# Swapping the operands of the query projection and building the identity first, in a decode attention kernel for one core

## The chip, the cores and the metric

The kernel runs on one core of a Trainium2 chip (trn2). The metric is the device time of one execution in microseconds (us), median over runs. A trace covers the "span" of the core, which is about 1.9 us shorter than the time. PE is the matmul engine, PEld its weight loads, DVE the vector engine, ACT the scalar engine, POOL GpSimd, SP the engine that issues the large loads. `SPq` lines are issues of DMA transfers. The traces also give the clock that PE was granted, as a share of full speed; here it lies between 0.50 ("the low clock" below) and 1.00. At the start of a trace it reads 1.00 although matmuls run slowly (last section); there "the low clock" means matmuls that run slowly, as where four K transposes take 1.09 us, against 0.64.

## The reference

Two independent attention decode steps (A over 8192 cached keys, B over the last 2048), one query token, batch 4, 32 query heads, 8 key/value heads of dimension 128, all bf16:

```python
q = (x @ wq).reshape(B, 1, 32, 128)           # x: [4, 1, 512], wq: [512, 4096]
scores = einsum(q, k) * 128 ** -0.5            # k, v repeated 4x over the heads
o = einsum(softmax(scores), v)
out = o.reshape(B, 1, 4096) @ wo               # wo: [4096, 512]
# the outputs of A and B are concatenated: [4, 1, 1024]
```

Every cached key and value, and every weight, is read from HBM once: 184.56 MB.

## The kernel before

The work is 20 "units" of 4 MB of K and 4 MB of V each: first four of B, then sixteen of A. K and V have two buffers each. For each unit PE transposes K (64 matmuls in 16 jobs), multiplies it with the query matrix RQ, and multiplies V with the exponentials. Ahead of this come the two query projections, problem 1 (B) first. Their weights lie in the V buffers until V is loaded. The parts that matter here:

```python
def pe_job_QP(P, i):                  # projection, a quarter of the heads
    def fn(pe):
        for hl in range(HQJ):         # 8 heads
            hq = i * HQJ + hl
            for c in range(DC):       # 4 chunks of 128
                pe.matmul(out=bk[:, hl * Bn:(hl + 1) * Bn], lhsT=wv[:, c, hq * DH:(hq + 1) * DH],
                          rhs=xT[:, P, c, :], start=(c == 0), stop=(c == DC - 1))
    # ... ACT copies bk to QT; pe_job_perm then reorders QT, and ACT writes RQ

# POOL, in this order: masks; memsets of ones, RQ, OT_sb, oacc, PT, Wo_sb; ident, identf; permE
def pool_setup1(pool):
    pool.affine_select(out=ident[:, :], in_=onesb[:, :], ...)     # waits for all the memsets

# SP: the loads of K and V
w = [("T", tjob_idx[(u - 2, 4 * q + 3)])] if u >= 2 else []       # K of unit u, piece q (B)
w = [("otr", u - 2)] if u >= 2 else [("T", tjob_idx[(1, 1)])] if u else [("T", qp_idx[(1, NQP - 1)])]   # V of unit u
# ... order on SP: WQ B, WQ A, K0, K1, V0, K2, V1, K3, V2, ...
```

SP issues loads in a fixed order (K0 is the K of unit 0, and so on). V0 waits for the end of problem 1's projection. K2 waits, in four pieces, for the transposes of unit 0. V1 waits for a transpose of unit 1. So a late PE makes SP issue late.

Of the kernel before, what the change touches and what calls it, by code (L numbers as in the profile page):

```python
# [9 lines left out]
ACTF = mybir.ActivationFunctionType  # L10
# [4 lines left out]
def bass_concat_heads__gqa_block_cached__sliding_block_cached__decode_kernel(  # L15
# [15 lines left out]
    Bn, _, D = A_x.shape  # L31
    _, HKV, SK, DH = A_k_cache.shape
    HQ = A_wq.shape[1] // DH
# [3 lines left out]
    DC = D // 128  # L37
# [6 lines left out]
    TC = NT // NC  # L44
    assert REP == 4 and Bn == 4 and HKV == 2 * NSEG and W == 64 * TS and NT == 128
    BIG = 1.0e30
    NQP = 4
    HQJ = HQ // NQP
    scale = float(DH) ** -0.5
    NKT = 4  # L50
    NW = 64
# [20 lines left out]
    with ExitStack() as es:  # L72
# [8 lines left out]
        def sm(name):  # L81
# [5 lines left out]
        Wo_sb = sb("Wo_sb", [128, C, D], BF16)  # L87
        Wl_sb = sb("Wl_sb", [128, C, D], BF16)
        ident = sb("ident", [128, 128], BF16)
        onesb = sb("onesb", [128, 128], BF16)  # L90
        identf = sb("identf", [128, 128], F32)
        onesf = sb("onesf", [128, 128], F32)
        RQ = [sb("RQ%d" % P, [128, Bn, NSEG, 2, 2 * C], BF16) for P in range(2)]
        RQc = sb("RQc", [128, 2, NSEG, 2, 2 * C], BF16)
        permE = sb("permE", [128, 2, 2, 64], BF16)
# [12 lines left out]
        xT = sb("xT", [128, 2, DC, Bn], BF16)  # L108
        QT = sb("QT", [128, 2, Bn, HQ], BF16)
        Dt = sb("Dt", [128, NT * C], F32)  # L110
        PT = sb("PT", [128, 2, NT * C + NW], BF16)
# [6 lines left out]
        oacc = sb("oacc", [Bn, D], F32)  # L118
# [6 lines left out]

        names = ["k0", "k1", "kh", "v0", "v1", "vl0", "vl1", "vl2", "vl3", "vl4", "wl0", "wl1", "wl2", "wl3", "wl4", "wl5", "wl6", "wl7", "x0", "x1", "w0", "w1", "wo",
                 "out0", "out1", "out2", "Tq", "Td", "Ta", "S", "PV", "Ed", "Ea", "Eq", "vs", "sub", "exp", "otr", "otp",
                 "ocp", "Ef", "fin0", "fin1", "ar1", "SM", "msk", "pset", "setup", "pm0", "pm1", "oc", "ocB", "mk0", "mk", "mka", "perm", "rq"]
        sems = {n: sm("s_" + n) for n in names}

        K_sbf = K_sb.bitcast(F32)
# [1 line left out]
        jobs = []  # L133
        bank_last = {}
        follow = {}
        tjob_idx, qp_idx, xt_idx, perm_idx, ot_idx, ol_idx, opj_idx = {}, {}, {}, {}, {}, {}, {}

        def sem_of(key):
            t = key[0]
# [26 lines left out]
        def op(eng, fn, waits=(), inc=None, bump=None):  # L166
            waits = list(waits)
            if not (eng == "pe" and turn[0] is not None):
                waits = [w for w in waits if w is not None]
            t = turn[0] if eng == "pe" or (eng in ("dve", "act") and turn[0] is not None and turn[0] >= T0P) else None  # L170
            plan[eng].append(dict(fn=fn, waits=waits, inc=inc, turn=t, bump=bump))

        def add(d):
            op(d["eng"], d["fn"], waits=d["waits"], inc=d["inc"])

        def new_job(kind, eng):
            idx = len(jobs)
            step = 2 if kind == "OT" else 1
            bank = (jobs[-1]["bank"] + step) % NBK if jobs else 0
            jobs.append(dict(kind=kind, idx=idx, bank=bank, prev=bank_last.get(bank), eng=eng, turn=turn[0]))  # L180
            bank_last[bank] = idx
            return idx

        def bankfree(idx):
            p = jobs[idx]["prev"]
            if p is None or (jobs[idx]["turn"] is not None and jobs[p]["turn"] is None):
                return None
            return ("F", p)

        def kbank(idx):  # L190
            return KTB[jobs[idx]["bank"]]
# [21 lines left out]
        def pe_job_QP(P, i):  # L213
            idx = qp_idx[(P, i)] = new_job("QP", "act")
            bk = kbank(idx)
            wv = wq_view(P)

            def fn(pe):
                ins = None
                for hl in range(HQJ):  # L220
                    hq = i * HQJ + hl
                    for c in range(DC):
                        ins = pe.matmul(out=bk[:, hl * Bn:(hl + 1) * Bn], lhsT=wv[:, c, hq * DH:(hq + 1) * DH],
                                        rhs=xT[:, P, c, :], start=(c == 0), stop=(c == DC - 1))
                return ins
            op("pe", fn, waits=[("WQ", P), ("E", xt_idx[P]), bankfree(idx)], inc=("T", idx))

            def efn(act):
                return act.activation(out=QT[:, P, :, i * HQJ:(i + 1) * HQJ],
                                      in_=bk[:, 0:HQJ * Bn].rearrange("p (h b) -> p b h", b=Bn), func=ACTF.Copy)  # L230
            add(dict(eng="act", fn=efn, waits=[("T", idx)], inc=("E", idx)))

        def pe_job_perm(P):
            idx = perm_idx[P] = new_job("perm", "act")
            bk = kbank(idx)

            def fn(pe):
                ins = None
                for e in range(2):
                    ins = pe.matmul(out=bk[:, e * Bn * HQ:(e + 1) * Bn * HQ],  # L240
                                    lhsT=permE[:, e, :, :].rearrange("p t i -> p (t i)"),
                                    rhs=QT[:, P, :, :].rearrange("p b h -> p (b h)"), start=True, stop=True)
                return ins
            op("pe", fn, waits=[("E", qp_idx[(P, NQP - 1)]), ("perm",), bankfree(idx)], inc=("T", idx))

            def efn(act):
                ins = None
                for tl in range(2):
                    ins = act.activation(
                        out=RQ[P][64 * tl:64 * tl + 64, :, :, :, C * tl:C * tl + C].rearrange("p b g e c -> p e (b g) c"),  # L250
                        in_=bk[64 * tl:64 * tl + 64, 0:2 * Bn * HQ].rearrange("p (e s c) -> p e s c", e=2, c=C), func=ACTF.Copy)
                return ins
            add(dict(eng="act", fn=efn, waits=[("T", idx)], inc=("E", idx)))

        def pe_filler(n):
            bank = (jobs[-1]["bank"] + 1) % NBK
# [34 lines left out]
        def pool_rq(u):  # L291
            un = units[u]
            w = [("E", perm_idx[un["P"]])]
            if un["P"] == 1:
                src = RQ[1][:, un["b"], :, :, :]
            else:
                src = RQ[0][:, un["b"], un["gp"]:un["gp"] + 1, :, :].broadcast_to([128, NSEG, 2, 2 * C])
            return dict(eng="pool", fn=lambda pool: pool.tensor_copy(out=RQc[:, u % 2, :, :, :], in_=src), waits=w, inc=("rq", u))
# [202 lines left out]
        def pool_otp(tn):  # L501
# [5 lines left out]
                w.append(("otr", 2 * tn - 2))  # L507
            return dict(eng="pool", fn=lambda pool: pool.tensor_copy(out=OTp[:, :, :], in_=OT_sb[:, P, q, :, :]), waits=w, inc=("otp", tn))

        def pool_mask0(pool):  # L510
            mkv = MK[:, :].rearrange("p (g s h) -> p g s h", g=NSEG, s=2)
            pool.memset(mkv[0:64, :, 0, :], 0.0)
            pool.memset(mkv[0:64, :, 1, :], -BIG)
            pool.memset(mkv[64:128, :, 0, :], -BIG)
            return pool.memset(mkv[64:128, :, 1, :], 0.0)
        op("pool", pool_mask0, inc=("mk0",))

        def pool_mask1(pool):
            pool.memset(MASK[0][0:64, 0:REP], 0.0)
# [2 lines left out]
            return pool.memset(MASK[0][64:128, REP:C], 0.0)  # L522
        op("pool", pool_mask1, inc=("mka",))

        def pool_setup0(pool):
            pool.memset(dummy[:, :], 0.0)
            pool.memset(onesf[:, :], 1.0)
            pool.memset(onesb[:, :], 1.0)
            pool.memset(RQ[0][:, :, :, :, :], 0.0)
            pool.memset(RQ[1][:, :, :, :, :], 0.0)  # L530
            pool.memset(OT_sb[:, :, :, :, :], 0.0)
            pool.memset(oacc[:, :], 0.0)
            pool.memset(PT[:, :, :], 0.0)
            return pool.memset(Wo_sb[:, :, :], 0.0)
        op("pool", pool_setup0, waits=[("mk0",), ("mka",)], inc=("pset",))

        def pool_setup1(pool):
            ins = pool.affine_select(out=ident[:, :], in_=onesb[:, :], pattern=[[1, 128]],
                                     compare_op=AluOpType.is_equal, fill=0.0, base=0, channel_multiplier=-1)
            ins = pool.affine_select(out=identf[:, :], in_=onesf[:, :], pattern=[[1, 128]],  # L540
                                     compare_op=AluOpType.is_equal, fill=0.0, base=0, channel_multiplier=-1)
            return ins
        op("pool", pool_setup1, waits=[("pset",)], inc=("setup",))

        def pool_perm(pool):
            ins = None
            for e in range(2):
                for tl in range(2):
                    ins = pool.tensor_copy(out=permE[:, e, tl, :], in_=ident[:, :].rearrange("p (i e) -> p e i", e=2)[:, e, :])
            return ins  # L550
        op("pool", pool_perm, waits=[("setup",)], inc=("perm",))
        def dve_msk(dve):
            idv = ident[0:NR, 0:NR].rearrange("p (h b) -> p h b", h=C)
            dve.tensor_reduce(out=MSK[:, :], in_=idv, axis=AX.X, op=AluOpType.max)
# [22 lines left out]
        for P in (1, 0):  # L577
            pe_job_xT(P)
            for i in range(NQP):
                pe_job_QP(P, i)  # L580
            pe_job_perm(P)
        op("pe", None, waits=[("E", perm_idx[0]), ("setup",), ("msk",)])
        op("dve", None, waits=[("msk",)])
        add(pool_rq(0))

        LA = 3
# [348 lines left out]
```

## Time and profile before

| | |
|---|---|
| time, median of 3 runs | 439.83 us (439.62 to 440.04) |
| span of the traced run | 437.9 us |
| bytes moved, mean rate | 184.75 MB, 422 GB/s |
| PE, DVE, ACT, POOL busy | 83%, 48%, 44%, 7% |

The page of the kernel before: engines, then 40 slices of 10.9 us each (a digit is the busy share in tenths), then what the DMA moved.

```profile
PE 363.9 (83%) x7174; PEld 336.5 (77%) x7184; DVE 209.5 (48%) x404; ACT 193.3 (44%) x217; POOL 29.1 (7%) x96
PE   0078898998998959896989598969878895989986
DMA  8999999999999999999999999999999999999996
GB/s 336 431 412 418 419 419 419 421 445 406 450 431 431 417 445 431 434 428 431 434 434 428 432 434 431 428 434 431 406 456 431 431 428 434 431 431 410 446 407 253
```

The DMA row is full between its first and last slice; no engine is. PE does nothing in the first two slices, and that is where the change works.

The timeline of the kernel before, first 38 us (start us, duration us, engine, line, operation, output and inputs, how many merged, and in brackets the idle time before and what ended it):

```profile
5.43 3.51 POOL L534 MEMSET Wo_sb<- 128x4096 bf16 x1
20.41 0.28 POOL L538 TENSOR_SCALAR_AFFINE_SELECT ident<-onesb 128x128 bf16<-128x128 bf16 x1 [11.47 <-issue]
21.10 0.26 PE L200 MATMUL KT<-ident,x_sb 4*128 4x4 bf16 x4 [21.10 <-POOL identf L540]
21.72 3.55 PE L223 MATMUL KT<-xT,V_sb 128*128 128x4 bf16 x128 [0.36 <-ACT xT L206]
27.12 3.66 PE L223 MATMUL KT<-xT,V_sb 128*128 128x4 bf16 x128 [0.94 <-ACT xT L206]
34.09 3.67 PE L279 MATMUL KT<-identf,K_sb 128*128 128x128 f32 x16 [2.62 <-DMA K_sb<-in_B_k_cache_dram]
37.82 1.09 PE L279 MATMUL KT<-identf,K_sb 128*128 128x128 f32 x4
```

POOL stands idle for 11.47 us before the identity. PE cannot start until that is there. Both projections are over by 31 us. Then PE waits for the first K, which lands at 34 us. So even here something slower than the projections ends the start-up: the loads.

The queue of SP in the same trace, from the first V load on:

```profile
25.31 3.80 SPq L568 DMA_DIRECT2D V_sb<-in_B_v_cache_dram  x4
37.79 10.35 SPq L568 DMA_DIRECT2D K_sb<-in_B_k_cache_dram  x4
55.68 2.48 SPq L568 DMA_DIRECT2D V_sb<-in_B_v_cache_dram  x4
58.27 6.93 SPq L568 DMA_DIRECT2D K_sb<-in_B_k_cache_dram  x4
```

The third of these lines is V1. When it is issued, 25.17 MB (WQ twice, K0, K1, V0, K2, at 4.19 MB each) have been issued and, summing the windows of 5 us, about 22.4 MB have moved. The remaining 2.7 MB last some 6.5 us at 420 GB/s. That is the stock that the DMA lives on while it waits for PE.

### The profile page before, as it was taken

To read this page: it belongs to the slowest core of one execution; us is meant where nothing else is said; L and a number is where in the kernel's file an instruction comes from. 1 tells how busy PE (TensorE), PEld (TensorE's weight loads), DVE (VectorE), ACT (ScalarE), POOL (GpSimd) and SP (SyncE) were. 2 spreads that over 40 slices of the span, in tenths; PEclk is the share of its full clock that TensorE was granted. 3 is DMA by queue.
4 is the path that set the end of the run, shared out by engine and by line. 5 is a ranking of instruction groups with operands and counts; after the bars stand their busy time and mean duration, and the time that the engine had idled before them with its cause. 6 is when DMAs were issued, how large, how long until landed. Compare 5 with 4: busy or idle time off the path is not lost.

```text
span 437.9 us, 15510 instructions
## 1 busy us (share of the span) xinstructions
PE 363.9 (83%) x7174; PEld 336.5 (77%) x7184; DVE 209.5 (48%) x404; ACT 193.3 (44%) x217; POOL 29.1 (7%) x96
## 2 busy tenths in 40 slices
PE   0078898998998959896989598969878895989986
PEld 0068897997997959795979588968868795979975
DVE  0004455664565634463456247625644563556641
ACT  1033473563653625372635264534534361635630
POOL 7110000000000000000000000000100000000000
PEclk9999999999999997999899699989998999999999
DMA  8999999999999999999999999999999999999996
GB/s 336 431 412 418 419 419 419 421 445 406 450 431 431 417 445 431 434 428 431 434 434 428 432 434 431 428 434 431 406 456 431 431 428 434 431 431 410 446 407 253
DMA packets 12500, 184.75 MB, mean 422 GB/s; under 512 B 1428, under 2 KB 2504, under 8 KB 2760
## 3 DMA queue, kind: packets, MB, share of 16 engines
q1 hardware_dynamic: 12400, 184.56, 99.2%
q8 instruction: 8, 0.13, 0.1%
q14 instruction: 4, 0.03, 0.0%
q0 software_dynamic: 64, 0.02, 0.0%
q10 hardware_dynamic: 24, 0.01, 0.0%
HBM read 184.56 MB, written 0.01 MB: 421 GB/s over the span
## 4 chain that ended last, share of the span: by engine, by line
PE 51%; DMA 43%; issue 2%; DVE 1%; SPq 1%; PEld 1%; PEldq 0%
DMA K_sb<-in_A_k_cache_dram 29%; PE KT L279 25%; PE OT L326 10%; DMA K_sb<-in_B_k_cache_dram 7%; DMA V_sb<-in_A_v_cache_dram 7%; PE SB L310 4%; PE SA L310 4%; PE KT L384 4%; SPq L568 1%; PE SA L338 1%; DVE oacc L392 1%; PE KT L326 1%; PEld OT L326 1%; PE KT L262 0%; DVE OS L489 0%
## 5 line engine op out<-in xcount | busy, mean ns | idle before, releaser
L279 PE MATMUL KT<-identf,K_sb 128*128 128x128 f32 x1280 | 206.2, 294 | 44.0 <-DMA K_sb<-in_A_k_cache_dram 33.0
L288 ACT ACTIVATE KT_sb<-KT 128x1024 bf16<-128x1024 bf16 x160 | 163.4, 1025 | 121.1 <-PE KT L279 121.1
L279 PEld LDWEIGHTS KT<-identf,K_sb 128*128 128x128 f32 x1280 | 146.2, 148 | 49.4 <-DMA K_sb<-in_A_k_cache_dram 34.2
L287 DVE COPY KT_sb<-KT 128x512 int32<-128x512 int32 x160 | 110.5, 690 | 131.2 <-PE KT L279 129.9
L326 PE MATMUL OT<-PT,V_sb 128*128 128x64 bf16 x2560 | 78.1, 193 | 2.5 <-issue 1.4
L326 PEld LDWEIGHTS OT<-PT,V_sb 128*128 128x128 bf16 x2560 | 75.9, 98 | 2.7 <-issue 1.5
L457 ACT ACTIVATE PT<-Dt 128x512 bf16<-128x512 f32 x40 | 24.6, 632 | 84.1 <-DVE Dt L446 84.1
L310 PEld LDWEIGHTS SA<-RQc,KT_sb 128*128 128x128 bf16 x1280 | 56.7, 98 | 2.3
L310 PEld LDWEIGHTS SB<-RQc,KT_sb 128*128 128x128 bf16 x1280 | 51.1, 97 | 7.9 <-issue 4.4
L310 PE MATMUL SA<-RQc,KT_sb 128*128 128x16 bf16 x1280 | 56.2, 170 | 0.0
L310 PE MATMUL SB<-RQc,KT_sb 128*128 128x16 bf16 x1280 | 52.8, 170 | 0.0
L408 DVE TENSOR_REDUCE M<-SB 128x8 f32<-128x512 f32 (+1 forms) x20 | 13.8, 692 | 49.9 <-PE SB L310 49.9
L429 POOL PARTITION_ALL_REDUCE MB<-M1m x20 | 7.7, 387 | 333.3 <-DVE M1m L422 333.3
L384 PE MATMUL KT<-Wo_sb,OL 128*4 128x512 bf16 x80 | 18.9, 379 | 0.0
L200 PE MATMUL KT<-ident,x_sb 4*128 4x4 bf16 x8 | 0.6, 170 | 21.1 <-POOL identf L540 21.1
L200 PEld LDWEIGHTS KT<-ident,x_sb 4*128 4x128 bf16 x8 | 0.4, 113 | 21.3 <-issue 21.3
L464 DVE TENSOR_REDUCE LB<-SA 128x8 f32<-128x512 f32 (+1 forms) x20 | 13.7, 684 | 2.8 <-PE SA L338 2.8
L446 DVE TENSOR_TENSOR Dt<-SA,MBm 128x512 f32<-128x512 f32 x20 | 13.8, 692 | 0.7
L355 DVE TENSOR_TENSOR ORx<-KT,MSK 32x1024 bf16<-32x1024 bf16 x10 | 12.1, 1211 | 3.7 <-PE KT L350 3.7
L408 DVE TENSOR_REDUCE M<-SA 128x8 f32<-128x512 f32 (+1 forms) x20 | 13.6, 681 | 0.0
L446 DVE TENSOR_TENSOR Dt<-SB,MBm 128x512 f32<-128x512 f32 x20 | 13.6, 681 | 0.0
L338 PE MATMUL SA<-PT,onesb 128*128 128x128 bf16 x168 | 12.7, 218 | 0.0
(74 smaller groups left out, 119.7 us busy)
## 6 DMA issues: line engine op xcount, KB each, us to landing
K_sb<-in_A_k_cache_dram SPq DMA_DIRECT2D x15, 4096.0 KB, 22.6
V_sb<-in_A_v_cache_dram SPq DMA_DIRECT2D x15, 4096.0 KB, 30.6
K_sb<-in_B_k_cache_dram SPq DMA_DIRECT2D x16, 1024.0 KB, 22.0
V_sb<-in_B_v_cache_dram SPq DMA_DIRECT2D x16, 1024.0 KB, 18.4
V_sb<-in_B_wq_dram SPq DMA_DIRECT2D x1, 4096.0 KB, 12.5
V_sb<-in_A_wq_dram SPq DMA_DIRECT2D x1, 4096.0 KB, 22.0
Wo_sb<-in_B_wo_dram SPq DMA_DIRECT2D x4, 1024.0 KB, 11.9
K_sb<-in_A_k_cache_dram SPq DMA_DIRECT2D x2, 2048.0 KB, 18.9
```

The lines of the kernel that those rows point to most:

```text
L279: ins = pe.transpose(out=bkf[:, pi * 128:(pi + 1) * 128], in_=K_sbf[:, slot, t0:t0 + 2, :].rearrange("p t d -> p (t d)"), identity=identf[ ...
L287: return e.tensor_copy(out=KT_sb.bitcast(I32)[:, tj % NKT, :], in_=bkf.bitcast(I32)[:, :])
L288: return e.activation(out=KT_sb[:, tj % NKT, :], in_=bk[:, :], func=ACTF.Copy)
L310: ins = pe.matmul(out=stb[:, t % NTH * C:(t % NTH + 2) * C], lhsT=ktv[:, pi, :, e], rhs=RQc[:, u % 2, t // TS, e, :], start=(e == 0), stop ...
L326: ins = pe.matmul(out=otb[:, s * NW:s * NW + w], lhsT=V_sb[:, slot, t, :], rhs=PT[:, slot, t * C:t * C + w], start=(j == 0), stop=(j == n ...
L338: ins = pe.matmul(out=SA[u % 2][:, s * NM:(s + 1) * NM], lhsT=onesb[:, :], rhs=PT[:, u % 2, c0:c0 + NM], start=(i == 0), stop=(i == n - 1))
L355: return dve.tensor_tensor(out=ORx[:, :, :, :], in0=bk[0:NR, 0:128].rearrange("p (i o r) -> p r o i", o=1, r=C).broadcast_to([NR, C, C, 12 ...
L384: ins = pe.matmul(out=bk[0:Bn, 0:D], lhsT=OL[:, i, :], rhs=Wo_sb[:, i, :], start=(i == 0), stop=(i == C - 1))
L408: return dve.tensor_reduce(out=M1[:, h * n:(h + 1) * n].rearrange("p (s h) -> p s h", h=C), in_=bank[:, :].rearrange("p (s j h) -> p s h j ...
L446: return dve.tensor_tensor(out=Dt[:, h * NTH * C:(h + 1) * NTH * C].rearrange("p (s j h) -> p s j h", s=Sh, h=C), in0=bank[:, :].rearrange ...
L457: return act.activation(out=PT[:, u % 2, a:b], in_=Dt[:, a:b], func=ACTF.Exp, scale=scale)
L464: return dve.tensor_reduce(out=LB[:, 0:n].rearrange("p (s h) -> p s h", h=C), in_=SA[u % 2][:, 0:NSEG * NM].rearrange("p (s j h) -> p s h ...
```

## The change

It has two parts. The projection takes x as the stationary operand and streams the weights, 512 columns at a time: 32 matmuls instead of 128 for a problem. The result then lies with the batch on 4 partitions and must be turned, by 32 small matmuls with the identity. POOL builds the identity before it fills anything else, so that PE can begin earlier.

```diff
-    NQP = 4
+    NQP = HQ * DH // 512
@@ pe_job_QP
-                for hl in range(HQJ):
-                    hq = i * HQJ + hl
-                    for c in range(DC):
-                        ins = pe.matmul(out=bk[:, hl * Bn:(hl + 1) * Bn], lhsT=wv[:, c, hq * DH:(hq + 1) * DH],
-                                        rhs=xT[:, P, c, :], start=(c == 0), stop=(c == DC - 1))
+                for c in range(DC):
+                    ins = pe.matmul(out=bk[0:Bn, 0:512], lhsT=xT[:, P, c, :], rhs=wv[:, c, i * 512:(i + 1) * 512],
+                                    start=(c == 0), stop=(c == DC - 1))
...
+        def pe_job_QT(P):                  # new, between the projection and the permutation
+                for hq in range(HQ):
+                    ins = pe.matmul(out=bk[:, hq * Bn:(hq + 1) * Bn], lhsT=qrow[:, hq * DH:(hq + 1) * DH], rhs=ident[0:Bn, 0:Bn],
+                                    start=True, stop=True)
... POOL's order
-    masks, dummy, onesf, onesb, RQ, OT_sb, oacc, PT, Wo_sb, ident, identf, permE
+    dummy, onesf, onesb, ident, identf, permE, RQ, OT_sb, oacc, PT, Wo_sb, masks
... ACT's write of RQ and PE's start on K now wait for the fills
```

More of the change, by code (lines that the diff above doesn't have):

```diff
@@ L46, in bass_concat_heads__gqa_block_cached__sliding_block_cached__decode_kernel @@
     BIG = 1.0e30
-    NQP = 4
-    HQJ = HQ // NQP
+    NQP = HQ * DH // 512
     scale = float(DH) ** -0.5
@@ L127, in bass_concat_heads__gqa_block_cached__sliding_block_cached__decode_kernel @@
                  "out0", "out1", "out2", "Tq", "Td", "Ta", "S", "PV", "Ed", "Ea", "Eq", "vs", "sub", "exp", "otr", "otp",
-                 "ocp", "Ef", "fin0", "fin1", "ar1", "SM", "msk", "pset", "setup", "pm0", "pm1", "oc", "ocB", "mk0", "mk", "mka", "perm", "rq"]
+                 "ocp", "Ef", "fin0", "fin1", "ar1", "SM", "msk", "ones", "pset", "setup", "pm0", "pm1", "oc", "ocB", "mk0", "mk", "mka", "perm", "rq"]
         sems = {n: sm("s_" + n) for n in names}
@@ L135, in bass_concat_heads__gqa_block_cached__sliding_block_cached__decode_kernel @@
         follow = {}
-        tjob_idx, qp_idx, xt_idx, perm_idx, ot_idx, ol_idx, opj_idx = {}, {}, {}, {}, {}, {}, {}
+        tjob_idx, qp_idx, qt_idx, xt_idx, perm_idx, ot_idx, ol_idx, opj_idx = {}, {}, {}, {}, {}, {}, {}, {}
         def sem_of(key):
@@ L228, in efn, with fn @@
             def efn(act):
-                return act.activation(out=QT[:, P, :, i * HQJ:(i + 1) * HQJ],
-                                      in_=bk[:, 0:HQJ * Bn].rearrange("p (h b) -> p b h", b=Bn), func=ACTF.Copy)
+                return act.activation(out=Wl_sb[0:Bn, i, :], in_=bk[0:Bn, 0:512], func=ACTF.Copy)
+            add(dict(eng="act", fn=efn, waits=[("T", idx)] + ([("T", qt_idx[1])] if P == 0 else []), inc=("E", idx)))
+        def pe_job_QT(P):
+            idx = qt_idx[P] = new_job("QT", "act")
+            bk = kbank(idx)
+            qrow = Wl_sb[0:Bn, :, :].rearrange("p c n -> p (c n)")
+            def fn(pe):
+                ins = None
+                for hq in range(HQ):
+                    ins = pe.matmul(out=bk[:, hq * Bn:(hq + 1) * Bn], lhsT=qrow[:, hq * DH:(hq + 1) * DH], rhs=ident[0:Bn, 0:Bn],
+                                    start=True, stop=True)
+                return ins
+            op("pe", fn, waits=[("E", qp_idx[(P, NQP - 1)]), bankfree(idx)], inc=("T", idx))
+            def efn(act):
+                return act.activation(out=QT[:, P, :, :], in_=bk[:, 0:HQ * Bn].rearrange("p (h b) -> p b h", b=Bn), func=ACTF.Copy)
             add(dict(eng="act", fn=efn, waits=[("T", idx)], inc=("E", idx)))
@@ L243, in fn @@
                 return ins
-            op("pe", fn, waits=[("E", qp_idx[(P, NQP - 1)]), ("perm",), bankfree(idx)], inc=("T", idx))
+            op("pe", fn, waits=[("E", qt_idx[P]), ("perm",), bankfree(idx)], inc=("T", idx))
             def efn(act):
@@ L252, in efn @@
                 return ins
-            add(dict(eng="act", fn=efn, waits=[("T", idx)], inc=("E", idx)))
+            add(dict(eng="act", fn=efn, waits=[("T", idx), ("pset",)], inc=("E", idx)))
         def pe_filler(n):
@@ L508, in pool_otp @@
             return dict(eng="pool", fn=lambda pool: pool.tensor_copy(out=OTp[:, :, :], in_=OT_sb[:, P, q, :, :]), waits=w, inc=("otp", tn))
-        def pool_mask0(pool):
-            mkv = MK[:, :].rearrange("p (g s h) -> p g s h", g=NSEG, s=2)
-            pool.memset(mkv[0:64, :, 0, :], 0.0)
-            pool.memset(mkv[0:64, :, 1, :], -BIG)
-            pool.memset(mkv[64:128, :, 0, :], -BIG)
-            return pool.memset(mkv[64:128, :, 1, :], 0.0)
-        op("pool", pool_mask0, inc=("mk0",))
-        def pool_mask1(pool):
-            pool.memset(MASK[0][0:64, 0:REP], 0.0)
-            pool.memset(MASK[0][0:64, REP:C], -BIG)
-            pool.memset(MASK[0][64:128, 0:REP], -BIG)
-            return pool.memset(MASK[0][64:128, REP:C], 0.0)
-        op("pool", pool_mask1, inc=("mka",))
         def pool_setup0(pool):
@@ L527, in pool_setup0 @@
             pool.memset(onesf[:, :], 1.0)
-            pool.memset(onesb[:, :], 1.0)
-            pool.memset(RQ[0][:, :, :, :, :], 0.0)
-            pool.memset(RQ[1][:, :, :, :, :], 0.0)
-            pool.memset(OT_sb[:, :, :, :, :], 0.0)
-            pool.memset(oacc[:, :], 0.0)
-            pool.memset(PT[:, :, :], 0.0)
-            return pool.memset(Wo_sb[:, :, :], 0.0)
-        op("pool", pool_setup0, waits=[("mk0",), ("mka",)], inc=("pset",))
+            return pool.memset(onesb[:, :], 1.0)
+        op("pool", pool_setup0, inc=("ones",))
         def pool_setup1(pool):
@@ L542, in pool_setup1 @@
             return ins
-        op("pool", pool_setup1, waits=[("pset",)], inc=("setup",))
+        op("pool", pool_setup1, waits=[("ones",)], inc=("setup",))
         def pool_perm(pool):
@@ L551, in bass_concat_heads__gqa_block_cached__sliding_block_cached__decode_kernel, with pool_zero, pool_mask0, pool_mask1 @@
         op("pool", pool_perm, waits=[("setup",)], inc=("perm",))
+        def pool_zero(pool):
+            pool.memset(RQ[0][:, :, :, :, :], 0.0)
+            pool.memset(RQ[1][:, :, :, :, :], 0.0)
+            pool.memset(OT_sb[:, :, :, :, :], 0.0)
+            pool.memset(oacc[:, :], 0.0)
+            pool.memset(PT[:, :, :], 0.0)
+            return pool.memset(Wo_sb[:, :, :], 0.0)
+        op("pool", pool_zero, inc=("pset",))
+        def pool_mask0(pool):
+            mkv = MK[:, :].rearrange("p (g s h) -> p g s h", g=NSEG, s=2)
+            pool.memset(mkv[0:64, :, 0, :], 0.0)
+            pool.memset(mkv[0:64, :, 1, :], -BIG)
+            pool.memset(mkv[64:128, :, 0, :], -BIG)
+            return pool.memset(mkv[64:128, :, 1, :], 0.0)
+        op("pool", pool_mask0, waits=[("pset",), ("perm",)], inc=("mk0",))
+        def pool_mask1(pool):
+            pool.memset(MASK[0][0:64, 0:REP], 0.0)
+            pool.memset(MASK[0][0:64, REP:C], -BIG)
+            pool.memset(MASK[0][64:128, 0:REP], -BIG)
+            return pool.memset(MASK[0][64:128, REP:C], 0.0)
+        op("pool", pool_mask1, inc=("mka",))
         def dve_msk(dve):
@@ L580, in bass_concat_heads__gqa_block_cached__sliding_block_cached__decode_kernel @@
                 pe_job_QP(P, i)
+            pe_job_QT(P)
             pe_job_perm(P)
-        op("pe", None, waits=[("E", perm_idx[0]), ("setup",), ("msk",)])
+        op("pe", None, waits=[("E", perm_idx[0]), ("pset",), ("msk",)])
         op("dve", None, waits=[("msk",)])
+        op("pool", None, waits=[("mka",)])
         add(pool_rq(0))
```

## The prediction

> **What bounds the kernel.** The DMA. The page reports 184.75 MB at a mean of 422 GB/s over 437.9 us; in the 40 slices DMA reads 9 everywhere but in the first and last, while PE is 83% busy. [...] The chain of waits alternates between K loads and PE, but the timeline shows K loads issued about 20 us before they land, behind other queued loads: the queue does not run dry. The two projections lie in the first 34 us, after which PE waits for K anyway (2.6 us idle before the first K transpose at 34.09 us, released by the K load).
>
> **What the change moves** (timeline, first 50 us).
> - GpSimd: the memsets end at 8.9 us, then 11.5 us of idle "issue" [...] until the identity at 20.41. After: [...] the identity comes at 13 to 14 us if it lasts as long. The displaced fills (7.4 us) end near 22 us, before RQ is written. The first WQ lands at 13.3 us, the second at 23.3 us, unchanged.
> - PE, removed: 128 matmuls of 4 columns a problem, 3.55 and 3.66 us. Added: 32 of 512 columns. The output projection of that shape takes 1.82 us for 8, so 7.0 to 7.3 us a problem when warm, twice the old cost. [...] K transposes go from 3.67 us for 16 to 0.49 us for 4 about 5 us after their start. So the first projection, cold at first, is an estimated 9 to 10 us.
> - Added: 32 small transposing matmuls, an estimated 1 to 1.5 us; one more evacuation round trip, about 0.5 us; eight 4x512 evacuations by ScalarE, an estimated 0.6 us each (4x256 took 0.374), hidden behind PE.
>
> Sum: problem 1 starts near 14 and is permuted by 26 us (before 26); problem 0 finishes near 38 us (before 32.3). The first K transposes start 3 to 4 us later than 34.09, but with a warm PE, which gives back about 3 us. Net near +1 us at unit 0.
>
> **How much is critical.** Almost nothing. The second V load, issued at 55.68 us after a transpose of unit 1, is the tightest: 25.2 MB had been issued, about 22.4 MB moved, so some 6.5 us of queue remained; +1 us fits in it, and so would +5. The first V load (25.31 us) moves by 2 us at most, with 7 MB queued. No byte is added or removed; the tail is untouched.
>
> **Predicted: 439.8 us**, 80% range 438.8 to 441.0. Faster by over 2%: 0.01; within 2%: 0.97; slower: 0.02.
>
> **What would show it.** Identity at 13 to 15 us; projection matmuls 0.22 us apart once warm, 7 us for problem 0; last RQ write and first K transposes near 38 us, at the warm rate; second V load issued within 3 us of 55.7; DMA at 9 in slices 2 to 39.
>
> **What would make it wrong.** If PE stays cold in the projections [...], the K transposes start near 48 us and the queue could run dry for some us around 53 us: up to +6 us. [...] A gain of more than 1 us would need DMA time that I read as full (374 GB/s at 20 to 25 us) to be recoverable.

The sum: problem 1 permuted by 26 us, problem 0 near 38, net near +1 us at unit 0, and 439.8 us. Of its terms, the 9 to 10 us of the first projection is the author's estimate: 7.0 to 7.3 us from the output projection (1.82 us for 8), plus some 2.5 us if PE is at first as slow as in the K transposes of the same trace (16 take 3.67 us at 34.09 us and 1.95 us at 54.57; four take 1.09 us at 37.82 us and 0.66 at 40.29; the 0.49 of the prediction is the same step in the chain of waits). That little DMA time was left rests on the DMA row alone. The identity at 13 to 14 us is an estimate from the idle 11.47 us, whatever their cause. The small matmuls and the round trip are estimates without a named source; in the trace of before, 128 matmuls of 4 columns take 3.55 us, which is 0.9 us for 32, and PE waits 0.29 us for the last copy of a projection's result. The 427 ns between weight loads in experiments 2 and 8 give 13.7 us for 32 matmuls.

## The result, and the profile after

| | before | after |
|---|---|---|
| time, median of 6 runs | 439.81 us (439.62 to 440.12) | 439.86 us (439.68 to 441.26) |
| ratio after / before | | 1.0008 (95%: 0.9994 to 1.0022) |
| span of the traced run | 437.9 us | 437.9 us |
| V1 issued at | 55.68 us | 56.79 us |

A ratio is the mean time of one kernel's fast runs over that of the other's in the same rounds, so it is not quite the ratio of the medians. Executions over 1.5% slower than the fastest of the same kernel are left out of the means.

The page of the kernel after, same rows:

```profile
PE 374.6 (86%) x7046; PEld 337.3 (77%) x7056; DVE 209.5 (48%) x404; ACT 201.6 (46%) x227; POOL 29.2 (7%) x96
PE   0787998998999869896989698969878895989986
DMA  8999999999999999999999999999999999999996
GB/s 336 431 412 424 417 424 415 422 444 407 450 431 431 418 444 431 431 431 431 431 434 428 429 434 431 428 434 431 412 450 431 434 428 431 434 431 416 440 410 247
```

PE does 10.7 us more work, and does it in slices that were empty. The DMA row is the same digit for digit.

The timeline of the kernel after, the lines that answer to those shown of before:

```profile
12.39 0.28 POOL L530 TENSOR_SCALAR_AFFINE_SELECT ident<-onesb 128x128 bf16<-128x128 bf16 x1 [11.21 <-issue]
13.71 8.52 PE L220 MATMUL KT<-V_sb,xT 128*4 128x512 bf16 x32 [0.37 <-ACT xT L205]
22.91 0.95 PE L237 MATMUL KT<-ident,Wl_sb 4*128 4x4 bf16 x32 [0.68 <-ACT Wl_sb L226]
25.68 7.07 PE L220 MATMUL KT<-V_sb,xT 128*4 128x512 bf16 x32 [0.94 <-ACT xT L205]
36.41 2.94 PE L292 MATMUL KT<-identf,K_sb 128*128 128x128 f32 x16 [1.38 <-ACT RQ L262]
39.37 9.94 SPq L584 DMA_DIRECT2D K_sb<-in_B_k_cache_dram  x4
39.40 1.09 PE L292 MATMUL KT<-identf,K_sb 128*128 128x128 f32 x4
56.79 2.48 SPq L584 DMA_DIRECT2D V_sb<-in_B_v_cache_dram  x4
```

The identity comes 8.0 us earlier. Problem 1's projection takes 8.52 us instead of 3.55, problem 0's 7.07 instead of 3.66. The two parts nearly cancel on PE. The bracket of the first K transposes is the line to look at: before, "DMA K_sb" ended PE's wait at 34.09 us; now "ACT RQ" ends it at 36.41 us. PE now comes after the load. It does not show in the time, because V1 is issued only 1.1 us later, with loads still queued.

### The profile page after: what moved, and what is told of

Same layout as the page of the kernel before. It is cut to its first block, busy times and chain, and to the rows that moved or that the text cites. A ratio compares the mean times of both kernels' runs of the same rounds, so it can differ in the third digit from the quotient of the medians.

```text
span 437.9 us, 15267 instructions
## 1 busy us (share of the span) xinstructions
PE 374.6 (86%) x7046; PEld 337.3 (77%) x7056; DVE 209.5 (48%) x404; ACT 201.6 (46%) x227; POOL 29.2 (7%) x96
## 4 chain that ended last, share of the span: by engine, by line
PE 55%; DMA 35%; issue 5%; DVE 1%; PEld 1%; SPq 1%; ACT 1%; POOL 0%; PEldq 0%; POOLq 0%
DMA K_sb<-in_A_k_cache_dram 28%; PE KT L292 25%; PE OT L339 10%; DMA V_sb<-in_A_v_cache_dram 7%; PE SB L323 4%; PE SA L323 4%; PE KT L397 4%; PE KT L220 4%; PE SA L351 1%; DVE oacc L405 1%; PE KT L339 1%; PEld OT L339 1%; SPq L584 1%; PE KT L237 0%; PE KT L275 0%
## 5 line engine op out<-in xcount | busy, mean ns | idle before, releaser
L220 PE MATMUL KT<-V_sb,xT 128*4 128x512 bf16 x64 | 15.6, 406 | 1.3 <-ACT xT L205 1.3
L477 DVE TENSOR_REDUCE LB<-SA 128x8 f32<-128x512 f32 (+1 forms) x20 | 13.7, 684 | 2.8 <-PE SA L351 2.8
L220 PEld LDWEIGHTS KT<-V_sb,xT 128*4 128x4 bf16 x64 | 5.6, 89 | 10.5 <-issue 3.1
L226 ACT ACTIVATE Wl_sb<-KT 4x512 bf16<-4x512 f32 x16 | 9.4, 587 | 7.7 <-PE KT L220 7.7
```

Of the source, the lines that this page charges most:

```text
L220: ins = pe.matmul(out=bk[0:Bn, 0:512], lhsT=xT[:, P, c, :], rhs=wv[:, c, i * 512:(i + 1) * 512], start=(c == 0), stop=(c == DC - 1))
L477: return dve.tensor_reduce(out=LB[:, 0:n].rearrange("p (s h) -> p s h", h=C), in_=SA[u % 2][:, 0:NSEG * NM].rearrange("p (s j h) -> p s h ...
```

## The experiments

Theory A: the time is set by the bytes, and start-up work on PE is free as long as SP issues its loads before the queue is empty. Rival B: the start-up is on the critical path, and the two halves of the change cancel by chance. The measured 1.0008 fits both. The diffs below are shortened to what they do.

### 1. The early identity alone

```diff
 kernel before
-    masks, memsets, ident, identf, permE
+    onesf, onesb, ident, identf, permE, memsets, masks      (waits as in the changed kernel)
```

> Early identity, old projection. Theory A (start-up work on PE is hidden behind the load queue): 439.8 us, ratio 1.000 within 0.002; identity near 12.4 us, second problem permuted near 28 us because its weights land at 23 us, first K transposes still near 34.1 us because K lands then. Rival B (the start-up is on the critical path and the earlier identity and the dearer projection cancel): 2 to 7 us faster.

Measured: 440.08 us (439.71 to 440.18, 5 runs), ratio 1.0006 (0.9993 to 1.0020). The timeline of this kernel:

```profile
10.76 0.28 POOL L517 TENSOR_SCALAR_AFFINE_SELECT ident<-onesb 128x128 bf16<-128x128 bf16 x1 [9.59 <-issue]
13.27 3.57 PE L223 MATMUL KT<-xT,V_sb 128*128 128x4 bf16 x128 [1.56 <-DMA V_sb<-in_B_wq_dram]
24.54 3.57 PE L223 MATMUL KT<-xT,V_sb 128*128 128x4 bf16 x128 [6.79 <-DMA V_sb<-in_A_wq_dram]
34.53 3.68 PE L279 MATMUL KT<-identf,K_sb 128*128 128x128 f32 x16 [5.74 <-DMA K_sb<-in_B_k_cache_dram]
```

The brackets of the three PE lines each name a DMA. An identity that is 9.7 us earlier only makes PE wait for the weights (13.27 and 24.54 us) and for K (34.53 us). Rival B's gain of 2 to 7 us is not there.

### 2. The new projection alone, with the late identity

```diff
 changed kernel
-    onesf, onesb, ident, identf, permE, memsets, masks
+    masks, memsets, ident, identf, permE                     (waits as in the kernel before)
```

> New projection, late identity. Theory A: first K transposes near 44.5 us, second V load issued near 65 us, when all that was issued before it (25.2 MB) has moved by about 62 us: the load queue runs dry once for 2 to 5 us, so 442 to 445 us and one hole in the DMA row near 62 to 67 us. Rival B: plus 8 us or more (448), one for one with the shift. A third view, that the slack is unlimited: 439.8.

Measured: 447.34 us (443.34 to 450.77, 4 runs; the longest is slow), ratio of the fast runs 1.0130 (1.0086 to 1.0175). The traced run: projections of 9.61 and 9.91 us, first K transposes at 47.55 us, V1 at 67.62 us, and a span of 445.2 us. Windows of 2 us in that trace (times, length, busy time of PE, PEld, DVE, ACT, POOL, granted clock, DMA share, GB/s):

```profile
54.00:56.00 2.00, 2.00 (x36) 1.88 (x34) 1.71 (x3) 1.25 (x2) 0.00 (x0) 1.00 0.71 274
56.00:58.00 2.00, 2.00 (x40) 1.93 (x37) 1.06 (x3) 1.29 (x2) 0.00 (x0) 1.00 0.68 233
58.00:60.00 2.00, 2.00 (x39) 1.97 (x37) 1.69 (x3) 1.33 (x3) 0.00 (x0) 1.00 0.83 311
64.00:66.00 2.00, 2.00 (x75) 2.00 (x72) 1.45 (x3) 0.46 (x1) 0.70 (x2) 1.00 0.71 274
66.00:68.00 2.00, 2.00 (x38) 2.00 (x35) 0.79 (x2) 1.14 (x3) 0.00 (x0) 1.00 0.09 33
68.00:70.00 2.00, 2.00 (x39) 1.97 (x38) 1.38 (x2) 1.71 (x3) 0.00 (x0) 1.00 0.57 193
```

In the trace of the kernel before, every such window from 48 to 80 us reads 406 to 426 GB/s. Here there are two shortfalls, where one was expected. The first is at K2, whose four pieces are issued only as unit 0 is transposed (51.23 to 61.6 us): 1.4 MB less than at 420 GB/s between 50 and 64 us, or 3.3 us. The second is just before V1 is issued at 67.62 us, where the queue runs dry (33 GB/s): 1.5 MB less between 64 and 70 us, or 3.6 us. So the start-up can be made critical, and the two halves of the change are not free of each other: the dearer projection needs the early identity. The cost, 5.7 us by the fast runs and 7.3 us in the traced one, is more than the 2 to 5 that theory A expected, and the fast runs alone scatter by 4.3 us. The projections were slower than reckoned; experiments 6 to 9 show why.

### 3. and 4. A plain delay ahead of the last write of RQ

The kernel before, with ACT copying 4096 columns over and over before it writes RQ of problem 0; nothing else is touched, and the result is right.

```diff
 kernel before, before ACT's write of RQ for problem 0
+            for d in range(2):          # experiment 4: range(5)
+                act.activation(out=KT_sb[all 4096 columns], in_=PT[...], func=Copy)
```

> Kernel before, with about 7 us of added ScalarE work ahead of the last write of RQ: first K transposes near 39.2 us, second V load near 60.7 us. Theory A: slack of about 6.5 us absorbs it, 439.8 to 440.5 us. Rival B: plus 5 us (445).

> Same with about 17 to 18 us of added work: first K transposes near 49.5 us, second V load near 71 us. Theory A: shift of 15 less slack of 6.5, so plus 8 to 11 us (448 to 451) with a hole in the DMA row of that size before 73 us. Rival B: plus 15 us (455). Unlimited slack: 439.8.

Measured: the short delay gives 440.09 us (439.59 to 440.62), ratio 1.0012 (0.9998 to 1.0026), K transposes at 39.29 us and V1 at 59.81 us, 4.1 us later than before. The long one gives 449.62 us (448.38 to 451.13), ratio 1.0232 (1.0208 to 1.0255), K transposes at 50.10 us and V1 at 68.95 us, 13.3 us later. Of 5 us nearly nothing is paid, of 16 us some 10: theory A, with a slack of about 6 us at the K transposes. Windows of the long delay:

```profile
52.00:54.00 2.00, 2.00 (x22) 1.98 (x21) 0.69 (x1) 1.52 (x2) 0.00 (x0) 1.00 0.09 37
66.00:68.00 2.00, 2.00 (x71) 2.00 (x68) 1.39 (x3) 1.14 (x2) 0.05 (x1) 1.00 0.38 147
68.00:70.00 2.00, 2.00 (x27) 1.99 (x26) 1.30 (x2) 1.14 (x3) 0.00 (x0) 1.00 0.00 0
```

There are two holes, as in experiment 2: one before K2 (issued at 53.50 us) and one before V1. Against 420 GB/s, 1.8 MB are missing between 50 and 64 us and 1.7 MB between 64 and 74 us, about 4 us each.

### 5. Fewer bytes in the steady part

```diff
 changed kernel, the seven 1 MB loads of Wo
-  dma(Wo_sb[:, :, :], src)
+  dma(Wo_sb[:, 0:1, :], src[:, 0:D])         # 128 KB; the result is wrong on purpose
```

> Changed kernel with the seven 1 MB loads of Wo cut to 128 KB each (wrong result on purpose): 6.4 MB less. Theory A (the bytes set the time in the steady part): minus 15 us at 422 GB/s, 424 to 428 us, DMA row still at 9. Rival (the steady part is set by the chain through PE, which holds over half of the chain of waits): under 4 us faster, and the DMA row falls below 9.

Measured: 425.10 us (424.96 to 427.78, 4 runs), ratio 0.9686 (0.9663 to 0.9709). The start-up is the same as in the changed kernel (V1 issued at 55.29 us), and the mean rate is 421 GB/s (184.75 MB less 6.4 over a span of 423.3 us), against 422 before. One of the four runs is 2.7 us longer than the other three; nothing says why. The gain is 14.6 us for 6.4 MB (7 x 7/8 MB), 440 GB/s. The chain of waits of the kernel before gives 51% to PE, but the DMA row reads 9 in all but the first and last slice, so that loads are queued in PE's share too; taking bytes away is what shortens the run.

### 6. Holding PE's clock up after the second projection

```diff
 changed kernel, problem 0 only
+    3 dummy 512-column matmuls          # fill the gap before the 32 small ones
     pe_job_QT(P)
+    2 dummy matmuls
     pe_job_perm(P)
+    7 dummy matmuls                     # fill the gap before K
```

> Changed kernel with 12 dummy 512-column matmuls on PE around the small phases of the second problem, to keep its clock up: first 16 K transposes in 1.8 us instead of 2.94, start near 36.6 us, second V load issued near 55.3 us instead of 56.8. Theory A: time 439.8, ratio 1.000 within 0.002, since the queue is full anyway. Rival B: 1 to 2 us faster.

Measured: 440.20 us (439.64 to 440.73, 5 runs), ratio 1.0012 (0.9999 to 1.0025). V1 is issued at 54.81 us, 2.0 us earlier than in the changed kernel's first trace, and K2 at 38.63 instead of 39.37; the first 16 K transposes took 2.15 us instead of 2.94. The traced span is 437.9 us as before: PE gained 2 us and the time did not. (In the trace of experiment 8's first batch the unaltered kernel reached 55.23 us without the dummies, so the gain is that of the clock and not always needed.)

### 7. The late identity with a clock that is held up

```diff
 kernel of experiment 2
+    42 dummy 512-column matmuls while PE waits for the identity
     and 3, 2 and 4 (problem 1) or 7 (problem 0) in the small phases
```

> New projection with the late identity, and dummy matmuls that raise PE's clock before the first projection and hold it through the small phases. If the clock, cold for 12 of 32 matmuls in each projection there, is what made the late version cost 4 to 11 us and scatter: projections 7.1 us each, first K transposes near 42.5 us at the fast rate, second V load near 61.5 us, 439.8 to 441 us and a spread under 1.5 us. If the late identity itself is the cost: 445 or more.

Measured: 441.65 us (439.86 to 443.22, 6 runs), ratio 1.0039 (1.0020 to 1.0059). Both projections took 7.07 us (9.61 and 9.91 in experiment 2, where the weight loads of each came 427 ns apart for its first 5 to 6 us), K transposes started at 42.62 us, V1 was issued at 60.24 us, and the traced span is 440.4 us. So of the 5.7 us that experiment 2 lost by its fast runs, about 70% (5.7 less 1.7 us) went with PE's clock; the spread expected (under 1.5 us) was missed, at 3.4 us. V1 is issued 4.6 us later than in the kernel before, and the rate of this run dips twice in its windows of 2 us, to 295 GB/s (64 to 66 us) and to 279 (132 to 136 us, where the next K and V of problem A are issued at 131.91 us, 7.2 us later than before). Between 60 and 70 us it moved 0.4 MB less than the kernel before, which is about 0.9 of the 2.5 us; by 140 us it was 1.0 MB behind. So 4.6 us at V1 is already at the edge. The first dip comes although loads were queued by then, and the DMA engines read as busy in it (a share of 0.97 at 295 GB/s, from 64 to 66 us); why the rate sags there stays open.

### 8. The changed kernel again, and again beside the next two

> The changed kernel again, unaltered: median within 0.5 us of 439.9. If its slack at the start is thinner, one or two runs 0.8 us or more above the others, as in the first six, where the kernel before shows none.

> The changed kernel unaltered, beside the two above: spans of 437.8 us in most runs, 439 us or more in about a third of them, those with the lower mean granted clock (0.946 to 0.953).

Measured: 440.56 us (439.67 to 442.12, 6 runs), ratio 1.0028 (1.0012 to 1.0043); and 440.51 us (439.73 to 442.28, 5 runs), ratio 1.0010 (0.9996 to 1.0024). All 17 runs of the changed kernel together have spans of 437.8 to 440.5 us, and seven are at 438.7 or more. The 29 runs of the kernel before that went with experiments have 437.6 to 438.2. The mean time of the 17 runs is 440.53 us, against 439.79 us for all 35 runs of the kernel before in these tables: the change costs about 0.7 us on average. In the last batch the spans and mean granted clocks were 440.5 at 0.946, 439.0 at 0.946, 438.7 at 0.946, 438.1 at 0.961 and 437.9 at 0.961. Over all 17, the seven long runs have 0.946 to 0.953 and the others 0.957 or more, but for one of 438.0 us at 0.949: the mean clock goes with the length without fixing it.

By luck the traced run of the last batch is one of the long ones, of 440.5 us:

```profile
13.94 9.79 PE L220 MATMUL KT<-V_sb,xT 128*4 128x512 bf16 x32 [0.95 <-DMA V_sb<-in_B_wq_dram]
27.17 10.00 PE L220 MATMUL KT<-V_sb,xT 128*4 128x512 bf16 x32 [0.94 <-ACT xT L205]
40.82 3.65 PE L292 MATMUL KT<-identf,K_sb 128*128 128x128 f32 x16 [1.38 <-ACT RQ L262]
61.99 2.81 SPq L584 DMA_DIRECT2D V_sb<-in_B_v_cache_dram  x4
```

The second batch's trace of the same kernel, a short run, has for the last two of these lines:

```profile
36.73 2.14 PE L292 MATMUL KT<-identf,K_sb 128*128 128x128 f32 x16 [1.38 <-ACT RQ L262]
55.23 2.48 SPq L584 DMA_DIRECT2D V_sb<-in_B_v_cache_dram  x4
```

Windows of the long run's trace, the granted clock being the third figure from the right:

```profile
29.00:31.00 2.00, 2.00 (x7) 0.55 (x5) 0.00 (x0) 0.81 (x2) 0.00 (x0) 0.50 1.06 442
35.00:37.00 2.00, 2.00 (x11) 0.68 (x8) 0.00 (x0) 1.37 (x3) 0.00 (x0) 1.00 0.99 414
61.00:63.00 2.00, 2.00 (x27) 1.99 (x26) 1.26 (x2) 1.00 (x2) 0.00 (x0) 1.00 0.61 246
63.00:65.00 2.00, 2.00 (x38) 1.97 (x37) 0.92 (x3) 1.72 (x3) 0.00 (x0) 1.00 0.87 287
```

The same kernel, the same matmuls: 10.00 us instead of 7.07 for the second projection. In the long run the clock fell to 0.50 in the small phases before it, at about 26 us, and 15 of its 32 weight loads come 427 ns apart; in the fast projection the matmuls start 216 ns apart on average (7.07 us for 32, less the 0.38 us that the last one takes). In the first trace of the changed kernel none of the second projection ran like this. V1 is issued 5.2 us later than there, at 61.99 us, and the DMA sags to 246 GB/s in that very window. Between 61 and 69 us it moved some 0.8 MB less than at 420 GB/s (four windows of 2 us at 246, 287, 389 and 344), or 2.0 of the 2.6 us that the span is longer.

### 9. The clock held up throughout, and a projection lengthened by what a low clock would cost

```diff
 changed kernel (first)
+    160 dummy 128-column matmuls of ones while PE waits for the identity
     and the dummy matmuls of experiment 7 in the small phases of both problems
 changed kernel (second), problem 0
+    every projection matmul is done twice (the result stays right)
```

> Changed kernel with dummy matmuls on PE while it waits for the identity and in all small phases. If the stray longer runs of the changed kernel (spans of 439.0 to 440.3 us beside 437.8) come from projections that stay at half clock for longer, this has none: both projections at about 7.1 us, all spans 437.7 to 438.3 us, mean ratio 1.000 to 1.001. If they have another cause (noise of the DMA, the chip), spans above 439 us stay.

> Changed kernel with every projection matmul of the second problem done twice, 7 us more on PE, which is what that projection would take entirely at half clock (13.7 us for 32). Queue slack of about 6 us: shift of the second V load to near 63 us, 441 to 443 us, the size of the stray runs. If no stray-run mechanism lies here: 440.

Measured, clock held up: 439.75 us (439.61 to 440.09, 5 runs), ratio 1.0001 (0.9987 to 1.0015); all five spans between 437.8 and 438.3 us. The second projection took 7.07 us and the K transposes 2.14 us for 16, and V1 was issued at 55.11 us. The first projection was not at 7.1 us, as expected, but at 8.59 us. PE had waited 1.83 us for its weights just before; that this is the reason is my guess, which no run here shows.

Measured, projection doubled (the 13.7 us expected from the low clock are 32 times the 427 ns of experiment 2): 445.26 us (443.12 to 446.61, 5 runs), ratio 1.0128 (1.0112 to 1.0144). The projection took 13.97 us, V1 was issued at 62.21 us, and the spans are 440.7 to 443.2 us. That is somewhat over the 441 to 443 expected. Part of the time is also outside the span (2.4 to 3.7 us in this kernel's runs, against 1.8 to 2.0 in nearly all others), which no run here explains.

### All traced runs of full loads in one table

V1's issue against the span of the same trace, in order (experiment 5, which moves fewer bytes, is left out):

| run | V1 issued, us | span, us |
|---|---|---|
| 6, clock held in problem 0 | 54.81 | 437.9 |
| 9, clock held throughout | 55.11 | 437.8 |
| changed kernel, second batch | 55.23 | 437.8 |
| 1, early identity alone | 55.27 | 437.9 |
| before | 55.68 | 437.9 |
| changed kernel, first batch | 56.79 | 437.9 |
| 3, short delay | 59.81 | 437.8 |
| 7, late identity, clock held | 60.24 | 440.4 |
| changed kernel, third batch | 61.99 | 440.5 |
| 9, doubled projection | 62.21 | 440.7 |
| 2, late identity | 67.62 | 445.2 |
| 4, long delay | 68.95 | 447.2 |

Up to 59.81 us the issue time does not matter at all; later, from 61.99 to 68.95 us, 7.0 us of delay cost 6.7. V1 stands here for the whole late start: in runs 2 and 4 K2 is late as well (51.23 and 53.50 us, against 45.98 at most in the others), and about half of their loss lies at K2. Delays made by the identity, by the projection, by ACT and by the clock give the same picture: nothing, then nearly one for one. (The run at 60.24 us lost the larger part of its time at a second tight place, near 132 us.) That is what theory A says and what rival B cannot say.

## Why the prediction was right or wrong

The time was predicted at 439.8 us within 438.8 to 441.0. The three medians of the changed kernel are 439.86, 440.56 and 440.51 us, and "within 2%" is clear. The reason given, that the DMA is the bound and its queue covers the shift, is what experiments 1, 3, 4, 5 and the table show. Within the sum, one step failed and one size was off, and that the total came out at +1 us is luck; the list says which.

- Identity at 13 to 14 us: it came at 12.39. POOL's idle time just before it is 9.59 to 11.47 us in the eight traces in which it was read, early or late.
- Projections at 9 to 10 and 7.0 to 7.3 us: 8.52 and 7.07. The price, taken from the output projection of the same shape (1.82 us for 8), was right at full speed, 216 ns apart. At first the matmuls came 427 ns apart (13.71 to 16.66 us).
- The small matmuls at 1 to 1.5 us: 0.95. An evacuation (ACT's copy of a projection's result out of PE's output memory) at 0.6 us: 0.59.
- "The first K transposes start 3 to 4 us later than 34.09": 2.3 us later, at 36.41.
- "But with a warm PE, which gives back about 3 us": this step failed in the run that was traced first. The K transposes started 2.3 us late and V1 was issued 1.1 us late, so 1.2 us were given back. The 16 transposes took 2.94 us, against 2.14 in the traces where the clock held, and the next four still ran at the low clock; the granted clock in that trace falls to 0.5 at about 37 us. Between 32.75 and 36.4 us PE has only 0.95 and 0.28 us of small matmuls, and in this trace the clock did not last through it. It is not always so: in the second batch's trace of the unaltered kernel the same 16 transposes took 2.14 us after the same gap, and V1 was issued at 55.23 us: 2.6 us late at K, 0.5 us early at V1, so that there the 3 us were given back. In the first trace the net shift of V1 was still the +1 us predicted, since the start was less late than reckoned: two errors that cancel.
- "+1 us fits in it, and so would +5": +1 and +4.1 fit; at +4.6 (experiment 7) about 0.9 us was lost at V1, and at +6.3 (the third batch) 2.0 us. The slack of 6.5 us worked out from bytes was too large by some 2 us; the rate sagged with loads still queued (295 GB/s from 64 to 66 us in experiment 7).
- "If PE stays cold in the projections ... up to +6 us" stood under what would make it wrong. It happens, in part, in 7 of 17 runs, for 0.8 to 2.6 us. The prediction took it for something that either happens or not; it differed from run to run (the second projection took 7.07, 7.07 and 10.00 us in the three traces of the changed kernel). Hence longer single runs (to 442.28 us) lie outside the range although the medians lie in it. The trace of one long run shows the slow projection directly; that it is behind every long run is inferred from their low granted clocks, with the exception named in experiment 8, and from the ten runs of experiments 6 and 9 with dummy matmuls, none of which has a span above 438.4 us.

No kernel here beats the one before. The best form of the change is that of experiment 9, which holds the clock up, and it is level with it: there is nothing to win at the start as long as the bytes set the time.

## What to carry to other kernels

Before costing a change at the start of a load-bound kernel, find the next load whose issue waits for that work and count the bytes still queued at that moment; then do the same for the loads after it, since a longer delay meets more than one. Here a delay of V1 by 4.1 us of a reckoned 6.5 was free, from 61.99 to 68.95 us 7.0 us of delay cost 6.7, and an identity 9.7 us earlier earned nothing (experiment 1). Here 128 short matmuls took 3.55 to 3.66 us in each of the four traces that have them, while the 32 long ones took 7.07 to 10.00 us, with the clock. With such a spread, run the kernel often enough to see the tail, not only the median. When two edits come together, run each alone: here the early identity alone gained nothing, the new projection alone cost 5.7 us, and the pair cost 0.7 us on average.

## What else the traces showed

- How long the low clock lasted differed between traces of the same kernel: the first projection ran at it for 3.0 us in one and 5.5 us in another (13.71 to 16.66 us; 13.94 to 19.44 us; about 7 and 13 matmuls 427 ns apart), and the second for 0 and 5.9 us. A gap of a few us with little matmul work kept the clock in one run and lost it in another: the 16 K transposes after the same gap took 2.14, 2.94 and 3.65 us in the three traces of the changed kernel. The long run's span was up to 2.6 us longer.
- In experiment 4 the 16 K transposes, after 19.6 us of idle PE and with nothing else running on it, took 3.37 us (3.65 in experiment 2, wholly at the low clock), and the next four, at 53.51 us, 0.63 us against 1.09 us at the low clock. So PE went from the low to the full clock with only these f32 transposes running.
- The idle time before the first identity instruction was 9.59 to 11.47 us in the eight traces in which it was read. The profile names no releaser for it ("issue"), and no run here shows its cause. In the kernel before, the DMA engines were busy all the while (a share of 1.00 and 423 GB/s from 9 to 20 us).
- The mean DMA rate of the kernel before is 422 GB/s; single slices of 10.9 us read up to 456 GB/s, which no run here explains. The rate sagged before a queue was empty (295 GB/s in one window of 2 us of experiment 7, with over 4 MB issued and not yet moved).
- The granted clock of the trace of the kernel before reads 1.00 at 37 to 39 us while four K transposes take 1.09 us, and still 1.00 when four take 0.64 us. The column of the changed kernel reads 1.00 from 13 to 17 us, while the matmuls of the first projection start 427 ns apart; its first reading below 1.00 is near 37 us. So a 1.00 ahead of the first lower reading did not mean full speed.
